# ScalarE casts one half of batch 0's last values, and the first 600 items of an attention-and-MLP kernel stand in a new order

## The chip, the cores and the metric

The kernel runs on one core of a Trainium2 chip. The core has five engines that run side by side, each with its own queue of instructions: TensorE (PE in the profile, its weight loads PEld), VectorE (DVE), ScalarE (ACT), GpSimd (POOL) and SyncE (SP), which here only issues transfers. An engine works through its queue in order; an instruction that waits for another engine or for a transfer holds up everything behind it on its own engine. The metric is the time of the whole program on the chip in microseconds (us), as the median of several runs.

## The reference: what is computed

Attention of 4 batches with 8 heads, 768 positions and head size 64, followed by a two-layer MLP over the 3,072 resulting rows of 512 numbers.

```python
scores = q @ k.T / sqrt(64)          # per batch and head
# retrieval heads (0, 2, 6): causal mask
# the other five heads: causal, and the key is one of the first 4 (sinks)
#                       or at most 63 positions back (window)
a = softmax(scores masked)
x = (a @ v), heads side by side       # 3072 x 512
h = x @ w_in                          # 512 -> 2048
g = max(h, 0) + alpha * min(h, 0)
out = g @ w_out                       # 2048 -> 512
```

Inputs and output are 32-bit floats; the kernel multiplies in bf16.

## The kernel before

**Segments.** A segment n (0 to 15) is one pair of heads of one batch: batch n // 4, pair n % 4 of (2, 6), (1, 5), (0, 4), (3, 7). Each half hh (0 or 1) of a segment is one head. The MLP works on 8 token tiles t (512 and 256 rows of each batch in turn), so t = 0 and 1 belong to batch 0, 2 and 3 to batch 1, and so on.

**Items.** The program is a list of 1,076 named items, `ORDER`, written out at the top of the file. The last loop of the kernel calls them one by one, and this alone sets the order of instructions on every engine's queue. No scheduler moves anything. The names, with the engine that does the work:

- `Lq`, `Lk`, `Lv` n: loads of queries, keys and values. SP issues them, apart from a few. Four buffers each, so a load waits until the segment four before it has been cast.
- `Cq`, `Ck`, `Cv` n: casts to bf16. The strings `CQ`, `CK`, `CV` name the engine by segment (P for POOL, A for ACT, V for DVE). Segment 3's values are cast by halves, `Cv3.0` and `Cv3.1` (`cast_v_head`, line 341 on); for heads that are not retrieval heads `sinks` (line 301 on) then copies the 4 sink rows to the other tiles.
- For n < 8, `Tq`, `Tk` transpose on PE and `tq`, `tk` move the result to `qT` and `kT` (DVE for the first keys, ACT from segment 4 on). For n >= 8, `Dq` (line 322) and `Dk` (line 338) let a transfer do the transpose; SP issues them.
- `S` n.hh.m: scores on PE (lines 413, 423, 430). `s`: the exponential on ACT. `m`: the mask on DVE, where the scores hold none already.
- `A` n.hh: weights times values on PE (line 552). `a`: division by the sum on DVE (lines 562 and 563), into `xn`.
- `X` n: transpose of `xn` into `xT`: on PE with a copy `x` by DVE (line 582) for batch 0 and segment 15, and otherwise by a transfer that SP issues (line 571).
- `P` t.f: first MLP layer on PE (line 597), reading all four parts of `xT` in the order of the pairs. For some, the four are split (`P0.f.0` to `.2`). `p`: relu of the negative on ACT (line 602), into one of three `neg` buffers. `g`: the rest of the activation on DVE (line 609).
- `O` t.s.u: quarter u of the second layer on PE (line 617). `o`: copy by ACT (line 623) and write by a transfer (line 627; POOL issues it for t < 6).
- `wi`, `wo`: loads of the MLP's weights, issued by POOL. `nms`, `nmr`, `nr`, `ns`: masks, made by POOL. `kz`, `vz`, `sz`, `so`, `ro`, `near`, `nz`, `kfz`, `qz`, `vo`, `one`, `zero`: fills, most by DVE. `warm`: matmuls on zeros (line 687).

**Banks.** PE writes to 8 banks. `take` picks the bank at build time, the one given back longest ago among those allowed; an item then waits until the former user's reader (`s`, `p` with `g`, `a`, `tk`, `o`) has let go of it.

**Bursts.** From segment 4 on, score matmuls that stand near one another in the list are collected and emitted together; large bursts alternate between the two halves on the two halves of the array (line 430), small ones use the whole array (line 423).

Of the kernel before, what the change touches and what calls it, by code (L numbers as in the profile page):

```python
# [23 lines left out]
one p0.1 g0.1 P0.2.2 Lq6 Lv7 p0.2 P0.0.2 P1.14 p1.14 g1.2 g1.14 Ck5.0 Ck5.1 nr Tk5 tk5.1 P0.3.2 tk5.0 g0.2 p0.0 g0.0
p0.3 g0.3 P0.12 p0.12 g0.12 p0.13 g0.13 P0.14 kfz1 P1.8 P0.8 wo0 p0.8 g0.8 P0.10 Ck7.1 S5.1.1 s5.1.1 P0.15 p0.15 wo1
wo2 wo3 ns p1.8 g0.15 g1.8 P0.11 p0.11 p0.14 g0.14 p0.10 S5.0.0 Lv5 P0.7 g0.10 P0.6 Ck6.1 P0.4.0 Lq7 P0.4.1 Lk8 Ck6.0
s5.0.0 p0.7 S5.0.2 s5.0.2 Cq4 Tq4 tq4 g0.11 P0.4.2 P0.9 nz0 Ck7.0 S5.1.0 p0.9 g0.9 P1.4 s5.1.0 p1.4 Lv6 S4.0.1 Cq6
m12.1.2 P0.5.0 s4.0.1 P0.5.1 P0.5.2 P1.12 m5.0.0 g1.4 S4.0.3 g0.7 p0.4 p0.5 m5.1.0 g0.4 g0.5 Cv5 P1.10 S5.0.1 p1.10
s5.0.1 near0 p0.6 g0.6 O0.1.0 Tq6 s4.0.3 m4.0.3 Tk6 tk6.1 tk6.0 O0.2.0 P1.6 p1.6 m5.0.1 Tk7 tk7.1 Lv4 S4.0.2 O0.2.1
g1.6 ro1 tq6 p1.12 s4.0.2 tk7.0 O0.1.1 O0.2.2 O0.1.2 g1.10 S4.0.4 S4.0.0 S5.1.2 g1.12 S4.0.5 S4.1.4 S4.1.0 s4.0.4  # L30
s4.0.0 m5.1.1 m4.0.4 s4.1.0 m4.1.0 m5.0.2 O0.1.3 s5.1.2 O0.3.0 O0.2.3 Cq7 m5.1.2 Ck8 Tq7 near1 A5.1 o0.1 S6.1.0 s4.1.4
s6.1.0 O0.3.1 a5.1 s4.0.5 O0.3.2 O0.3.3 m4.0.1 m4.0.5 Cv4 tq7 S7.0.0 S6.0.5 S7.1.1 S4.1.1 Lk9 Lk10 Lq9 o0.2 o0.3
S4.1.3 S7.0.1 A5.0 s4.1.1 s7.0.0 m4.0.0 a5.0 X5 A4.0 s7.0.1 Lk11 s7.1.1 a4.0 s4.1.3 O1.1.0 m4.1.3 Cv7 s6.0.5 m7.0.0
m7.1.1 Lq8 S7.1.0 S6.0.4 S7.0.2 S4.1.5 S6.0.1 S7.1.2 S6.1.1 O1.1.1 Cv6 s7.1.0 O1.0.0 s4.1.5 m7.0.1 s6.1.1 m4.1.5
m6.1.1 s7.1.2 m6.1.0 s7.0.2 m7.0.2 S6.0.2 S4.1.2 S6.1.2 S6.0.0 s6.0.4 s4.1.2 s6.0.1 s6.1.2 O1.0.1 m6.0.5 m7.1.0 m4.1.1
m4.1.4 m7.1.2 m6.1.2 S6.0.3 A4.1 s6.0.0 m6.0.0 m6.0.1 A7.1 O1.1.2 A6.1 s6.0.3 m6.0.4 m6.0.3 s6.0.2 a4.1 a6.1 A6.0 A7.0
a6.0 O1.1.3 O0.0.0 O0.0.1 O0.0.2 O1.0.2 m10.0.2 O1.0.3 O0.0.3 o0.0 X4 X6 a7.1 a7.0 X7 P2.9 P2.3 p2.9 P3.4 Ck9 Cq9 g2.9
P2.14 p2.14 g2.14 Cq8 p3.4 Lq10 Lq11 Dk8.0 P2.10 p2.10 Dk9.1 o1.0 p2.3 g2.3 g3.4 Dk8.1 P3.2 P3.14 P3.12 P2.8 Dq8 P2.1
P3.8 o1.1 p3.2 Dk9.0 Lv10 g2.10 Dq9 p3.14 P2.7 Ck10 g3.2 p3.12 g3.12 g3.14 P2.2 p2.2 g2.2 Cq10 Dq10 P2.11 p2.1 g2.1
p2.11 p2.8 g2.11 P3.6 P2.5 p2.5 g2.5 P2.13 p2.13 g2.8 g2.13 P2.0 p2.0 g2.0 p2.7 P3.0 p3.0 P2.4 S8.0.5 Lv8 Lv11 P2.15  # L40
P2.12 s8.0.5 Cq11 g3.0 p2.15 g2.7 g2.15 S8.0.0 p2.12 g2.12 Ck11 p3.6 S9.0.2 P2.6 p2.6 g3.6 s8.0.0 p2.4 g2.4 g2.6
s9.0.2 p3.8 P3.10 g3.8 p3.10 O3.0.0 O2.0.0 S8.1.5 s8.1.5 O3.0.1 O2.0.1 g3.10 m8.0.0 Cv8 S8.1.3 S9.0.0 S8.0.3 S9.1.1
S8.0.1 S9.1.0 s8.1.3 s9.1.0 s8.0.1 s9.0.0 s8.0.3 m8.0.3 m8.0.1 O2.0.2 O2.0.3 o2.0 Dk10.1 Lv9 m9.0.0 Cv9 m8.0.5 Dk11.0
m9.1.0 m9.0.2 S8.0.4 S9.0.1 S10.1.1 S8.1.4 Dq11 s8.1.4 Lq13 Lk13 O3.0.2 Dk10.0 s9.1.1 s10.1.1 s9.0.1 s8.0.4 O3.0.3
o3.0 Dk11.1 S10.1.0 S10.1.2 m9.0.1 S11.0.2 S9.1.2 S8.0.2 S11.0.0 s9.1.2 Cv10 m9.1.1 A9.0 s11.0.2 s10.1.0 O2.3.0 m9.1.2
A9.1 a9.0 a9.1 X9 s10.1.2 s11.0.0 O2.3.1 Lq15 Lv14 Lq12 S8.1.0 S11.0.1 S10.0.3 m10.1.0 s8.0.2 S10.0.1 S8.1.2 S8.1.1
S10.0.0 O2.3.2 s8.1.2 s8.1.0 m8.1.4 Cq13 s11.0.1 s8.1.1 m11.0.2 m10.1.2 m8.0.4 m11.0.0 A8.0 s10.0.0 m8.1.5 m10.1.1
O2.3.3 a8.0 S11.1.2 S10.0.4 S11.1.0 S10.0.5 S10.0.2 m8.1.3 m11.0.1 s10.0.3 s10.0.1 S11.1.1 s11.1.2 A10.1 s11.1.1
O2.2.0 O2.1.0 s10.0.4 m6.0.2 m10.0.1 Cv11 m8.1.1 m8.1.0 a10.1 m10.0.4 Ck13 m10.0.0 m11.1.2 A11.0 A8.1 O2.1.1 s10.0.2
s10.0.5 o2.3 s11.1.0 Dk13.0 m11.1.1 m10.0.3 m10.0.5 m11.1.0 A10.0 a11.0 a8.1 a10.0 O3.1.0 A11.1 Cq12 O2.2.1 O2.2.2  # L50
O2.2.3 a11.1 X8 O2.1.2 O3.1.1 O3.1.2 X10 o2.2 O3.1.3 O2.1.3 X11 P4.11 o2.1 P4.14 P5.14 p5.14 P4.4 P4.6 Lk12 P5.0 g5.14
Ck12 p4.4 p4.6 p4.11 P4.13 g4.6 p4.14 g4.11 Lq14 g4.14 P5.12 P4.5 P4.12 p4.13 Dq12 o3.1 p5.0 g4.13 Cq14 g5.0 Dk13.1
p4.5 g4.5 g4.4 Cv14 P4.9 p4.9 g4.9 P4.2 P5.2 Dq13 p5.12 g5.12 P4.10 p5.2 P4.8 P4.1 p4.12 g4.12 g5.2 p4.10 g4.10 Lv15
Dk12.0 Dk12.1 Lv12 p4.1 Lk14 Lv13 Lk15 g4.1 P4.7 P4.0 p4.2 g4.2 p4.8 g4.8 p4.0 p4.7 g4.7 P4.15 Cv12 S13.0.1 s13.0.1
S12.0.5 S12.0.3 P4.3 P5.4 g4.0 s12.0.3 p4.3 s12.0.5 S12.1.5 S12.0.1 S12.0.0 S13.1.1 s13.1.1 Dq14 g4.3 Cq15 Ck14
m12.0.3 O4.3.0 s12.1.5 s12.0.1 O4.3.1 O4.3.2 s12.0.0 p4.15 g4.15 P5.6 P5.10 S12.1.1 S12.0.4 S12.0.2 p5.4 S13.1.0 g5.4
p5.6 s12.0.4 Dk14.0 P5.8 s13.1.0 s12.0.2 p5.8 s12.1.1 m12.0.0 g5.6 O4.3.3 Ck15 p5.10 g5.8 m12.0.1 g5.10 m12.0.4 O5.1.0
Cv13 O5.1.1 O5.1.2 o4.3 Dk14.1 S14.1.1 S14.0.0 S12.1.4 S14.0.1 S14.1.0 S13.0.2 m12.1.1 s14.1.0 s13.0.2 O4.2.0 m12.0.5
A12.0 s14.0.1 s12.1.4 O5.1.3 Dk15.1 s14.1.1 Dk15.0 s14.0.0 a12.0 m14.0.1 Dq15 o5.1 O4.2.1 S13.1.2 S12.1.2 S14.1.2
S14.0.4 m13.1.0 m14.0.0 m13.0.1 S14.0.5 S13.0.0 O4.2.2 O4.2.3 s13.1.2 m13.1.2 m13.1.1 s13.0.0 s14.0.4 s14.0.5 m13.0.2  # L60
S12.1.0 m12.1.5 s14.1.2 S12.1.3 S15.0.0 S14.0.3 m13.0.0 A13.1 o4.2 s12.1.0 s12.1.2 A13.0 s15.0.0 O5.0.0 s12.1.3
s14.0.3 m14.0.4 Cv15 a13.1 O5.0.1 a13.0 S15.0.1 S15.0.2 m12.1.0 S15.1.0 S15.1.2 S15.1.1 S14.0.2 O4.1.0 s15.0.2 s15.1.0
m12.1.4 s14.0.2 s15.1.1 m14.1.1 m14.0.5 m14.1.2 m12.1.3 m14.1.0 A12.1 m14.0.3 A14.1 A14.0 a14.0 s15.1.2 a14.1 m15.0.2
s15.0.1 a12.1 O4.1.1 X13 O4.0.0 O4.0.1 O4.0.2 O4.0.3 m15.0.0 m15.1.1 O4.1.2 m15.0.1 m15.1.2 m15.1.0 A15.0 o4.0 A15.1
a15.0 O4.1.3 a15.1 O5.0.2 X15 O5.0.3 X14 x15 o4.1 o5.0 X12 P6.11 p6.11 P6.2 P6.15 P6.10 p6.10 P7.4 P6.0 P6.1 g6.11
g6.10 p6.1 P6.6 P7.8 p6.15 g6.15 g6.1 p6.0 g6.0 P6.5 p7.4 p6.5 p6.6 g7.4 g6.6 g6.5 P6.3 P6.12 P7.2 p6.3 p6.12 g6.12
p6.2 g6.2 P6.4 p7.8 P7.6 P6.14 g6.3 g7.8 p7.6 p6.4 g7.6 g6.4 P7.10 P6.7 P6.8 p6.8 p6.7 P7.0 P6.9 P6.13 g6.7 p7.2 g7.2
g6.8 p7.10 g7.10 p6.9 P7.14 O6.3.0 P7.12 p6.13 g6.13 p7.12 O6.0.0 O6.0.1 O6.1.0 p7.0 g7.0 g6.9 O6.3.1 O7.0.0 O6.3.2
O6.1.1 p7.14 p6.14 g6.14 g7.12 O6.3.3 o6.3 O6.0.2 O6.1.2 O6.1.3 o6.1 O6.0.3 o6.0 O6.2.0 O6.2.1 O6.2.2 O7.0.1 O7.0.2
O6.2.3 o6.2 m12.0.2 g7.14 L2 l2 O7.0.3 o7.0 L0 L1 l1 warm1 l0  # L70
""".split()


@with_exitstack
def kernel(
    ctx: ExitStack,
    tc: tile.TileContext,
    q: bass.AP,
    k: bass.AP,
    v: bass.AP,  # L80
    is_retrieval: bass.AP,
# [7 lines left out]
    nc = tc.nc  # L89
    B, H, S, D = q.shape  # L90
# [73 lines left out]
    NF, NK, NV, NR, NS = 4, 4, 5, 2, 3  # L164
# [175 lines left out]

    def cast_v_head(n, hh):
        vv = vb[n % NV]
        cast_of("PV"[hh])(vv[:, :, hh, 0:D], vf[n % NF][:, :, hh, :])  # L343
        sinks(n, vv.rearrange("p t h c -> p h t c"), [hh], (nc.gpsimd.tensor_copy, nc.vector.tensor_copy)[hh])

    def cast_v(n):
        vv = vb[n % NV]
# [499 lines left out]
```

## Time and profile before

| what | value |
|---|---|
| median of 3 runs | 228.47 us (227.57 to 230.39) |
| the profiled execution's own time | 229.76 us |
| its span, first to last instruction | 228.1 us |
| PE busy | 220.6 us (97%) |
| PE weight loads busy | 136.9 us (60%) |
| DVE busy | 151.5 us (66%) |
| ACT busy | 139.3 us (61%) |
| POOL busy | 46.2 us (20%) |
| PE P L597, share of the chain that ended last | 36% |
| PE P L617, share of it | 35% |
| PE P L552, share of it | 7% |
| granted clock of TensorE | 1.000 |

The time of an execution is a little longer than its span, since starting and ending the program count. Starts in the profile's views are microseconds from the span's start. In a row of the timeline the columns are start, duration, engine, line of the kernel, operation, tiles written and read, shapes, count, and in brackets the idle time ahead with what ended it. The letter q behind an engine's name stands for its queue, where transfers are issued. "A wait of PE" below is time in which PE's next instruction could not start.

### The profile page before, as it was taken

To read this page: it belongs to the slowest core of one execution; us is meant where nothing else is said; L and a number is where in the kernel's file an instruction comes from. 1 tells how busy PE (TensorE), PEld (TensorE's weight loads), DVE (VectorE), ACT (ScalarE), POOL (GpSimd) and SP (SyncE) were. 2 spreads that over 40 slices of the span, in tenths; PEclk is the share of its full clock that TensorE was granted. 3 is DMA by queue.
4 is the path that set the end of the run, shared out by engine and by line. 5 is a ranking of instruction groups with operands and counts; after the bars stand their busy time and mean duration, and the time that the engine had idled before them with its cause. 6 is when DMAs were issued, how large, how long until landed. Compare 5 with 4: busy or idle time off the path is not lost.

```text
span 228.1 us, 5213 instructions
## 1 busy us (share of the span) xinstructions
PE 220.6 (97%) x1977; PEld 136.9 (60%) x2005; DVE 151.5 (66%) x395; ACT 139.3 (61%) x284; POOL 46.2 (20%) x91
## 2 busy tenths in 40 slices
PE   7999979999999999999999999999999999999994
PEld 7989766476455656555556455556556555664454
DVE  5799757996549816999699219987586535966000
ACT  3688448899989128477994136787594236563311
POOL 5689736901040001000400001000110110000000
PEclk9999999999999999999999999999999999999999
DMA  6999999999998799989969899995921420000213
GB/s 193 312 249 219 278 224 280 198 196 244 203 262 165 97 188 207 212 190 188 251 155 194 197 251 174 211 158 107 132 93 38 116 95 0 0 4 0 89 68 120
DMA packets 95417, 37.39 MB, mean 164 GB/s; under 512 B 82440, under 2 KB 93600, under 8 KB 95392
## 3 DMA queue, kind: packets, MB, share of 16 engines
q1 hardware_dynamic: 89136, 27.73, 60.5%
q0 software_dynamic: 5792, 8.93, 17.4%
q10 hardware_dynamic: 464, 0.40, 0.5%
q8 instruction: 15, 0.25, 0.4%
q14 instruction: 10, 0.08, 0.1%
HBM read 27.71 MB, written 6.29 MB: 149 GB/s over the span
## 4 chain that ended last, share of the span: by engine, by line
PE 96%; DVE 2%; issue 1%; DVEq 0%
PE P L597 36%; PE P L617 35%; PE P L552 7%; PE P L430 4%; PE P L413 3%; PE P L687 3%; PE P L363 2%; PE P L636 2%; PE P L423 1%; DVE vb L343 1%; PE P L501 1%; PE P L577 1%; PE P L361 1%; PE P L462 0%; DVE xT L582 0%
## 5 line engine op out<-in xcount | busy, mean ns | idle before, releaser
L609 DVE SCALAR_TENSOR_TENSOR g<-neg,oma,P 128x256 bf16<-128x256 f32 (+1 forms) x128 | 70.9, 608 | 36.5 <-ACT neg L602 36.0
L597 PE MATMUL P<-xT,w_in_b 128*128 128x256 bf16 (+1 forms) x501 | 85.7, 325 | 0.6
L617 PE MATMUL P<-w_out_b,g 128*128 128x512 bf16 x351 | 83.1, 379 | 1.0 <-issue 0.2
L602 ACT ACTIVATE neg<-P 128x512 f32<-128x512 f32 x96 | 54.2, 600 | 26.3 <-PE P L597 18.2
L597 PEld LDWEIGHTS <-w_in_b 128*128 128x128 bf16 x512 | 49.5, 98 | 32.3 <-DVE g L609 0.2
L617 PEld LDWEIGHTS <-g 128*128 128x128 bf16 x368 | 33.9, 98 | 37.3 <-issue 1.0
L469 ACT ACTIVATE eR<-P 128x448 bf16<-128x448 f32 (+4 forms) x63 | 36.8, 633 | 5.8 <-PE P L430 2.5
L623 ACT COPY ot<-P 128x512 f32<-128x512 f32 x23 | 13.9, 605 | 37.1 <-PE P L617 32.3
L627 POOL DMA_DIRECT2D out_dram<-ot x18 | 10.3, 574 | 114.7 <-ACT ot L623 114.6
L517 ACT ACTIVATE eS<-P 128x352 bf16<-128x352 f32 x45 | 20.7, 487 | 3.4 <-PE P L430 3.0
L563 DVE TENSOR_TENSOR xn<-P,rcp 128x448 bf16<-128x448 f32 (+1 forms) x32 | 19.4, 608 | 1.1
L528 DVE TENSOR_TENSOR eS<-eS,ms_near 128x352 bf16<-128x352 bf16 x45 | 14.4, 334 | 0.6 <-ACT eS L517 0.5
L479 DVE TENSOR_TENSOR eR<-eR,mr_near 128x128 bf16<-128x128 bf16 (+5 forms) x54 | 10.8, 229 | 4.7 <-ACT eR L469 4.5
L562 DVE RECIPROCAL rcp<-P 128x7 f32<-128x7 f32 (+1 forms) x32 | 6.3, 197 | 10.1 <-PE P L552 9.9
L552 PE MATMUL P<-vb,eS 128*128 128x65 bf16 x260 | 10.8, 193 | 1.6 <-DVE vb L343 1.4
L552 PEld LDWEIGHTS <-eS 128*128 128x128 bf16 x260 | 9.6, 97 | 4.1 <-issue 2.5
L413 PE MATMUL P<-qT,kT 128*128 128x192 bf16 (+14 forms) x68 | 11.2, 251 | 0.2 <-DVE kT L386 0.2
L430 PE MATMUL P<-qT,kT 64*128 64x176 bf16 (+10 forms) x168 | 10.5, 251 | 0.0
L552 PE MATMUL P<-vb,eR 128*128 128x65 bf16 x276 | 10.5, 193 | 0.0
L430 PEld LDWEIGHTS <-kT 64*128 64x128 bf16 x168 | 6.7, 94 | 6.2 <-issue 5.5
L552 PEld LDWEIGHTS <-eR 128*128 128x128 bf16 x276 | 9.5, 97 | 1.3
L645 DVE COPY ot<-P 128x128 f32<-128x128 f32 x1 | 0.3, 291 | 14.3 <-PE P L636 14.3
(95 smaller groups left out, 180.1 us busy)
## 6 DMA issues: line engine op xcount, KB each, us to landing
out_dram<-ot POOLq DMA_DIRECT2D x18, 256.0 KB, 3.5
kf<-in_k_dram SPq DMA_DIRECT2D x21, 192.0 KB
qf<-in_q_dram SPq DMA_DIRECT2D x18, 192.0 KB
vf<-in_v_dram SPq DMA_DIRECT2D x14, 196.0 KB
qf<-in_q_dram SPq DMA_DIRECT2D x7, 384.0 KB
vf<-in_v_dram SPq DMA_DIRECT2D x12, 192.0 KB
w_in_b<-in_moe_w_in_dram POOLq DMA_DIRECT2D x8, 256.0 KB, 9.5
w_out_b<-in_moe_w_out_dram POOLq DMA_DIRECT2D x4, 512.0 KB, 12.2
```

The source lines that it names most:

```text
L413: nc.tensor.matmul(to, keys, queries, start=True, stop=stop)
L430: nc.tensor.matmul(to, keys[own], queries[own], start=True, stop=True)
L469: nc.scalar.activation(ebuf[n, hh][:, lo:hi].rearrange("p (x c) -> p x c", x=len(parts)), P[:, got[0]:got[0] + len(parts), 0:(hi - lo) // ...
L517: nc.scalar.activation(slots, sc[:, 0:352].rearrange("p (s c) -> p s c", c=176), AF.Exp, scale=scale)
L528: nc.vector.tensor_tensor(slots, slots, ms_near[:, 0:2, :] if m == 0 else ms_near[:, 1:3, :], op=ALU.mult)
L552: nc.tensor.matmul(pav[:, i, :], e[:, o:o + 128], vv[:, j, hh, 0:D + 1], start=(m == 0), stop=(m == len(terms) - 1))
L563: nc.vector.tensor_tensor(xn[n][:, 0:nt, D * hh:D * hh + D], pav[:, :, 0:D], rcp.to_broadcast([128, nt, D]), op=ALU.mult)
L597: nc.tensor.matmul(psg[:, w * i:w * (i + 1)], w_in_b[:, c, 128 * fb:128 * (fb + 1)], xT[:, c, o:o + w], start=(x == 0), stop=(x == 3))
L602: nc.scalar.activation(neg[t, f], bank(held["P", t, f][0]), AF.Relu, scale=-1.0)
L609: nc.vector.scalar_tensor_tensor(g_buf[t % 2][:, fb, 0:w], neg[t, f][:, c], oma[:, fb:fb + 1], bank(got[0])[:, c], op0=ALU.mult, op1=ALU.add)
L617: nc.tensor.matmul(bank(held["O", t, s][0]), g_buf[t % 2][:, f, 128 * s:128 * (s + 1)], w_out_b[:, f, :], start=(f == 0), stop=(f == 15))
L623: nc.scalar.copy(ot, bank(got[0]))
```

## The change

`Cv3.1`, the cast of the second half of segment 3's values, goes from VectorE to ScalarE, and with it the copy of that half's sink rows. The first half stays on GpSimd.

```diff
     def cast_v_head(n, hh):
         vv = vb[n % NV]
-        cast_of("PV"[hh])(vv[:, :, hh, 0:D], vf[n % NF][:, :, hh, :])
-        sinks(n, vv.rearrange("p t h c -> p h t c"), [hh], (nc.gpsimd.tensor_copy, nc.vector.tensor_copy)[hh])
+        copy = cast_of("PA"[hh])
+        copy(vv[:, :, hh, 0:D], vf[n % NF][:, :, hh, :])
+        sinks(n, vv.rearrange("p t h c -> p h t c"), [hh], copy)
```

The first 600 of the 1,076 items are the same items in another order; from the 601st on (`S8.1.4 Dq11 s8.1.4 Lq13 ...`) the list is unchanged. The order of the loads and transposes on SP's queue stays the same throughout. The stretches that the prediction speaks of, in the new order (first the start, then the end of batch 0's attention, then the middle of the first MLP phase, then the end of batch 1's attention, then the MLP of batch 1 with the first scores of batch 2):

```diff
+La zero busy warm4 warm0 sz0 ro1 vz2 Lq0.0 Lq0.1 Lk1 Lq1 Lk0 qz0 kz1 sz1 id kz0 Cq0.0 Tq0.0 Lk2 Ck0.0 Tk0.0 tk0.0 nmr
+warm2 Ck1.0 Cq0.1 Lv0 Lq2 tq0.0 kz2 S0.0.0 Lk3 Ck1.1 s0.0.0 kz3 Tk1 S0.0.1 s0.0.1 Cq1 warm6 warm7 Tq1 nms vz1 Ck0.1
...
+S3.1.1 x1 S3.0.1 s3.0.1 Ck4.1 s3.1.1 X2 x2 P0.1.0 A3.0 a3.0 P0.3.0 P0.1.1 P0.3.1 Cv3.1 A3.1 P0.0.0 m14.0.2 P0.0.1
+P0.2.0 P0.2.1 a3.1 X3 Tq5 tq5 Lq6 Lv7 Tk4 nz1 x3 P1.2 near0 P1.0 P0.1.2 tk4.0 p1.2 g1.2 wi3 near1 one nr p1.0 P0.3.2
...
+g0.13 p0.14 P0.10 p0.12 p0.15 Ck5.1 Ck6.0 g0.15 Ck5.0 Tk5 P0.11 tk5.1 tk5.0 P0.8 g0.12 wo0 wo1 wo2 Ck7.1 p0.10 g0.10
+P1.8 p1.8 P0.4.0 p0.8 S5.0.2 near2 s5.0.2 P0.4.1 P0.4.2 g0.14 P0.9 p0.11 g1.8 g0.8 wo3 S5.1.1 s5.1.1 g0.11 Ck6.1 p0.9
+Lv5 S5.1.0 p0.4 Lq7 Lk8 Lv6 P0.5.0 P1.12 ns Cq4 nz0 Tq4 s5.1.0 g0.9 Cv7 p1.12 tq4 g1.12 S5.0.0 s5.0.0 Cq6 P0.5.1
...
+S6.1.1 m7.0.1 s6.0.1 S6.0.0 m7.1.1 m6.0.1 s7.1.0 S4.1.2 S6.0.3 s6.0.3 m6.0.3 O1.1.3 O1.0.0 O1.0.1 s7.0.2 s6.1.1 Cv6
+s6.0.0 m6.0.0 m4.1.5 s4.1.2 m6.1.1 A4.1 m7.1.0 A7.1 m7.0.2 A7.0 X5 s6.0.2 s6.1.2 m6.1.2 A6.1 a4.1 Lk11 A6.0 O0.0.0
+O0.0.1 a6.1 O0.0.2 O0.0.3 a6.0 a7.0 O1.0.2 Lq8 a7.1 Cq8 X4 Ck9 X6 O1.0.3 X7 P2.2 P2.8 Lq10 Lq11 o0.0 P2.11 o1.0 Dk8.0
+p2.8 g2.8 P2.10 p2.10 p2.2 o1.1 P3.8 p3.8 g2.10 g3.8 P2.7 g2.2 P2.13 P2.5 p2.7 g2.7 p2.13 g2.13 p2.11 p2.5 g2.5 g2.11
+Dk9.1 Dk8.1 Dq8 Dk9.0 Ck10 P3.14 P2.4 p2.4 Cq10 g2.4 P2.9 p3.14 g3.14 S8.0.5 P2.3 p2.3 P2.6 p2.6 g2.6 P2.1 p2.1 g2.3
+Lv10 Dq9 Dq10 S9.0.2 p2.9 g2.9 g2.1 P3.0 p3.0 s8.0.5 P3.12 s9.0.2 P2.0 P3.10 g3.0 p3.12 P3.2 g3.12 p3.10 p2.0 Ck11
```

The same five stretches before:

```diff
-vz2 id busy warm4 warm0 warm5 vz0 qz0 Lq0.0 sz2 so2 Lq0.1 zero vz3 nms Lk1 Lq1 sz1 Cq0.1 nmr Ck1.1 kz1 La Lk0 Ck1.0
-kz0 Cq1 Cq0.0 Tq0.0 Ck0.0 Tk0.0 tk0.0 Lk2 Ck2.0 Lv0 warm2 tq0.0 S0.0.0 s0.0.0 qz S0.0.1 Tk1 warm3 warm6 vo kz2 Ck0.1
...
-a2.1 X2 x1 x2 m8.1.2 near2 Ck4.0 P0.0.0 wi2 s3.0.1 A3.0 Cv3.1 P0.3.0 a3.0 P0.2.0 P0.2.1 A3.1 Ck4.1 Lk7 Lk6 P0.1.0
-P0.1.1 P0.0.1 Tk4 tk4.0 Cq5 m14.0.2 a3.1 X3 nz1 tk4.1 x3 Tq5 P0.3.1 tq5 P1.2 p1.2 P1.0 p1.0 g1.0 P0.1.2 wi3 P0.13 Lq4
...
-s5.0.0 p0.7 S5.0.2 s5.0.2 Cq4 Tq4 tq4 g0.11 P0.4.2 P0.9 nz0 Ck7.0 S5.1.0 p0.9 g0.9 P1.4 s5.1.0 p1.4 Lv6 S4.0.1 Cq6
...
-m4.1.4 m7.1.2 m6.1.2 S6.0.3 A4.1 s6.0.0 m6.0.0 m6.0.1 A7.1 O1.1.2 A6.1 s6.0.3 m6.0.4 m6.0.3 s6.0.2 a4.1 a6.1 A6.0 A7.0
-a6.0 O1.1.3 O0.0.0 O0.0.1 O0.0.2 O1.0.2 O1.0.3 O0.0.3 o0.0 X4 X6 a7.1 a7.0 X7 P2.9 P2.3 p2.9 P3.4 Ck9 Cq9 g2.9
...
-p2.11 p2.8 g2.11 P3.6 P2.5 p2.5 g2.5 P2.13 p2.13 g2.8 g2.13 P2.0 p2.0 g2.0 p2.7 P3.0 p3.0 P2.4 S8.0.5 Lv8 Lv11 P2.15
-P2.12 s8.0.5 Cq11 g3.0 p2.15 g2.7 g2.15 S8.0.0 p2.12 g2.12 Ck11 p3.6 S9.0.2 P2.6 p2.6 g3.6 s8.0.0 p2.4 g2.4 g2.6
```

## The prediction

> **What bounds the kernel now.** I read the page first: the busy row of the matmul engine over 40 slices, then the chain that ended last.
>
> ```profile
> PE   7999979999999999999999999999999999999994
> PE 96%; DVE 2%; issue 1%; DVEq 0%
> ```
>
> TensorE (PE) is the bound. In the first half one slice stands out, the sixth (28.5 to 34.2 us), and the 2% of DVE in the chain is one cast. So only a wait of PE is worth anything, and any new wait of PE costs its full length. After 110 us, in the part of the order that the change leaves as it is, PE's rows have gaps of at most 0.43 us, so a delay at 110 us is carried to the end.
>
> Second, the timeline of VectorE (DVE), GpSimd (POOL) and PE around that slice. Columns: start, duration, engine, line, operation, tiles.
>
> ```profile
> 26.79 2.62 DVE L343 CAST vb<-vf 128x448 bf16<-128x448 f32 x1
> 29.44 0.36 DVE L306 COPY vb<-vb 4x192 f32<-4x192 f32 x1
> ...
> 27.00 0.52 POOL L328 CAST natm<-kf 128x384 bf16<-128x384 f32 x1
> 27.45 0.84 POOL L315 CAST natq<-qf 128x768 bf16<-128x768 f32 x1
> 28.22 0.91 POOL L288 MEMSET natk<- 128x960 f32 x1
> ...
> 26.45 0.56 PE L552 MATMUL P<-vb,eS 128*128 128x65 bf16 x13
> 26.84 1.24 PE L597 MATMUL P<-xT,w_in_b 128*128 128x512 bf16 x5
> 29.46 0.22 PE L552 MATMUL P<-vb,eS 128*128 128x65 bf16 x2 [1.38 <-DVE vb L343]
> 29.86 0.49 PE L552 MATMUL P<-vb,eS 128*128 128x65 bf16 x11 [0.18 <-DVE vb L306]
> ```
>
> The cast of segment 3's second half of values (item Cv3.1) took 2.62 us on DVE while POOL ran without a break. A DVE cast nearly as large, later and with POOL idle, is short:
>
> ```profile
> 46.23 0.62 DVE L328 CAST natm<-kf 128x384 bf16<-128x384 f32 x2
> ```
>
> Two in 0.62 us. PE waited: from the first of A3.1's 13 weight loads (27.71) to the item behind them are 2.45 us, against 0.58 for A3.0, the same 13 matmuls. The stall is 2.45 - 0.58 = **1.87 us**.
>
> Third, the queue of SyncE (SP), which I read because the new order asks for the scores of batch 2 sooner:
>
> ```profile
> 75.02 5.59 SPq L571 DMA_TRANSPOSE xT<-xn  x3
> 80.71 2.29 SPq L212 DMA_DIRECT2D qf<-in_q_dram  x4
> 83.10 4.65 SPq L338 DMA_TRANSPOSE kT<-natk  x3
> 87.84 1.24 SPq L322 DMA_TRANSPOSE qT<-natq  x1
> 89.13 1.34 SPq L338 DMA_TRANSPOSE kT<-natk  x1
> 90.53 0.57 SPq L246 DMA_DIRECT2D vf<-in_v_dram  x1
> 91.14 1.24 SPq L239 DMA_DIRECT2D vf<-in_v_dram  x1
> 92.43 1.00 SPq L242 DMA_DIRECT2D vf<-in_v_dram  x1
> 93.47 3.45 SPq L322 DMA_TRANSPOSE qT<-natq  x2
> ```
>
> The last of the three xT transposes (X7) is issued at 79.39. From there SP issues back to back until Dq9, the transpose of segment 9's queries (93.47, the first of the last row): no idle time over 0.1 us. When Dq9's data is complete, the GB/s of the transfers tells (93 to 98 us, 40 slices of 0.125 us):
>
> ```profile
> GB/s 189 197 199 189 209 264 172 129 225 228 221 217 229 215 213 215 223 205 223 217 223 240 98 4 96 287 91 0 0 0 0 104 211 229 219 203 199 209 156 33
> ```
>
> The stream stops after slice 27, at 96.4, and starts again with Dq10. So Dq9 is there at **96.4**. The scores S9.0.2, which read it, came far later, as the 128x448 group at 101.5:
>
> ```profile
> 99.81 1.89 PE L597 MATMUL P<-xT,w_in_b 128*128 128x512 bf16 x8
> 101.53 0.55 PE L423 MATMUL P<-qT,kT 128*128 128x448 bf16 x4
> ```
>
> **The change part by part, against the profiled execution's own 229.76 us** (span 228.1). The median of the runs, 228.47, is 1.29 lower; I add the difference to the median.
>
> *The cast on ScalarE (ACT).* It removes 2.62 + 0.36 from DVE and adds a 128x448 cast and a 4-partition copy to ACT. ACT's row for a 128x384 cast of the same types is 0.51, so 0.51 x 448/384 = 0.60; the copy lies between ACT's smallest copies (0.18) and DVE's 0.36; I take 0.3. ACT is idle for 5.23 us just there (26.36 to 31.58, in its timeline "5.23 <-PE P L363"), so 0.9 us is hidden; without that cover it would cost at most 0.9. Cv3.1 then ends at 26.3 + 0.9 = 27.2, and A3.1's turn on PE is at about 27.8: the stall is gone with 0.6 to spare. Next late is the path A3.1, its normalisation on DVE (0.86), X3, x3: with 0.3 us from PE to DVE, x3 ends at 30.9, and P1.2 starts at 30.7 instead of 32.14. That keeps 1.44 of the 1.87, since before, the items behind the stall ran without gaps.
>
> *The start.* The warm-up matmuls ahead of the first transposes drop from 40 to 36 (0.11 each there), so the transposes start about 0.4 earlier. But two small groups of warm-ups stand later instead (4 x 0.055 each), POOL does nms (five operations, 1.45) and kz3 ahead of Ck0.1, and ACT's exponentials (0.82 to 0.92 each) set the pace from 13 to 18 us. By hand I get S2.0.1 at 17.8 to 17.9, before 17.83. Taken as 0, bounds -0.4 and +0.3.
>
> *The order from 31 to 76 us.* P0.9's bank is that of g0.10, which now has ACT's six copies of tk5 (1.9) ahead of it: bank free at 42.9, P0.9's turn at 42.4, 0.4 to 0.5 lost. S5.1.0 and S4.0.2 wait for the evacuation of a score just issued, 0.2 each. The burst of scores before O1.1.3 waits for s7.1.0 on ACT, 0.7. So of 1.44 some 0.3 to 0.8 is left by 73 us; I take 0.5. One cast of DVE, Cv7, moves from 68.8 to 46.5, where its load has just landed: the 256-byte packets on SP's queue, of which Lv7 has 1,624 counted from 38.4, are through at 43.6, and its last completion comes at 44.7. The w_out transfers that slow this load start 0.9 earlier (their queue waits for the memset "one", which DVE reaches sooner), so the load may land at 45.5 to 47.5: 0 to 1 us, taken as 0.
>
> *X7.* A6.0's matmuls ended at 75.9. Now O1.1.3 (0.7) and A7.0 (0.4) stand ahead of them: 75.9 + 1.1 - 0.5 = 76.5. DVE then does a6.0, a7.0 and a7.1, 0.78 each, which before overlapped with PE: 76.5 + 0.3 + 2.4 = 79.2; or X6's issue (2.34 in its row) ends at 77.4 + 2.3 = 79.7. X7 goes out at about 79.5, before 79.39: shift **+0.1**, bounds -1.4 (the whole gain kept) and +0.8. So the gain of the cast is already used up here.
>
> *Scores of batch 2.* Before, S9.0.2 stood behind 22 groups P2/P3 and two small scores counted from P2's first (82.06): 101.54 - 82.06 = 19.48, or 0.86 a group. Now it stands behind 14 groups and one score: 14 x 0.86 + 0.35 = 12.4, due at 94.45. It is moved ahead by 7.1 us and had 101.54 - 96.4 = 5.1 of slack: PE waits 2.0 for Dq9. (S8.0.5 waits for its own queries, complete at 91.5 by the completion writes, about when its turn comes; that is part of the same wait.) Behind the waiting matmul stands all of PE's queue. Since this wait ends with SP's stream, and SP starts it at X7, the total is 2.0 + shift of X7 = 2.1. Against it: Dq9's issue lies 14.1 us behind X7's, of which Lv10's last two are 1.24 and 1.00, while such loads at 102.15 to 104.05 took 0.57 and 0.43; the output writes then in flight now go out earlier. Relief 0 to 1.3; I take 0.7.
>
> Sum: 2.0 + 0.1 - 0.7 = **+1.4 us**, so 231.2 on the profile's scale and 228.47 + 1.4 = **229.9** on the median's.
>
> **Rivals.**
> 1. *Faster.* Dq9 is there in time, and the cast's gain stays: 228.47 - 1.4 = 227.1. It decides at Dq9's landing: it must come by 93.0, 3.4 us earlier. For it: a bare stream (nine transposes at 1.23, loads at 0.45 to 0.6) would be 2 to 3 us shorter. Against: the loads ahead of Dq9 keep the transfers busy whatever SP does. Chance 0.22.
> 2. *Another hold of DVE.* Ck7.1, a cast like Cv3.1, moves from 43.0 to about 41.1, into the middle of POOL's 12 mask operations (ns, 3.6 us long). If it is held to their end at 43.0, DVE loses 1.9, P0.9's bank comes that much later, and the total is 1.4 + 1.9 = 3.3: 231.8. Against: in its old place, beside four of these operations, it took 0.39, alone 0.35. Chance 0.07. [...]
> 3. *Cv7 waits for its load*, 1 us on DVE and then PE: 230.9. Chance 0.06.
> 4. *The change doesn't do what it says*: ACT's cast is late behind s3.1.1, and the stall stays: 229.9 + 1.4 = 231.3. The 5.23 us idle speaks against it. Chance 0.05.
>
> My forecast has 0.60.
>
> **How the numbers follow.** Forecast's own range: -1.4 + 1.3 = about 1.3 below in the kindest case, and +0.7 (shift) +0.7 (no relief) above: 228.5 to 231.4. It and rival 1 have both signs: the range reaches down to 227.0 and up to 232.0, which takes in rivals 2 to 4. Two per cent is 4.6 us (a measurement of this kernel can tell no less from no change). Faster than 223.9 would need more than all of PE's waits ahead of 110 us, about 3.8 with the start: 0.02. Slower than 233.0: rival 2 with the whole wait, or a stall I missed: 0.08. Within: 0.90.
>
> **What would show it.** Right: no DVE cast near 26.8, ACT busy there, A3.1 without a stall, P1.2 near 30.7; X7's issue within 0.8 of 79.4; a PE wait of 1 to 3 us at line 423 near 95, ending as a qT transpose lands. Wrong: X7 well before 78.5, or S9.0.2 without a wait (rival 1); a DVE cast over 1 us near 41 (2) or 46.5 (3); PE idle near 28 (4).

## The result, and the profile after

The changed kernel takes **241.81 us** (median of 6 runs, 238.62 to 245.88) where the kernel before, in the same series, takes 228.68 (227.57 to 230.39). The ratio is 1.0524, with a 95% interval of 1.0469 to 1.0579: slower by 5%. Here and below, a ratio leaves out executions more than 1.5% above the fastest of their kernel (two of these six), while a median holds them all. The forecast was 229.9 with a range of 227.0 to 232.0, a change of under 1%, so the prediction was wrong. The profiled execution took 245.88 us (span 244.2) and is the longest of the six; the other five spans are 236.6 to 242.4. In all six the mean granted clock is below 1 (0.978 to 0.993), so each ran in part at a lower clock; the profiled one shows next where, and the lengths given here are its own. Lines of the changed file are one higher than before (343 is now 344, 597 is 598).

First the page of the changed kernel: PE's busy row, the granted clock, and the chain that ended last.

```profile
PE   8899999933999999979997999999999999999995
PEclk9999999995899999999997999999999999999999
PE 73%; DMA 15%; DVE 4%; SPq 3%; ACT 2%; issue 1%; POOL 1%; DVEq 0%; ACTq 0%
```

Before, the chain was 96% PE and every digit of PE's row but three was a 9. Now two slices (48.8 to 61.1 us) are at 3, with a clock that falls to half in the second of them, and 15% of the chain are transfers. Which ones, the list of the chain's longest pieces tells (start, length, what):

```profile
38.02 18.55 DMA vf<-in_v_dram
```

That is a load of values, the third of the four that make up Lv7; SP begins to issue it at 38.02, and it is complete at 56.57. PE's own waits in the changed kernel (total us, times, longest):

```profile
PE P L424 <- DVE g L610: 7.5, 1, 7.5
PE P L424 <- DMA qT<-natq: 2.4, 2, 1.8
PE P L431 <- DMA kT<-natk: 1.6, 1, 1.6
...
PE P L414 <- DVE qT L288: 0.6, 1, 0.6
PE P L553 <- POOL vb L349: 0.6, 1, 0.6
```

The second row is the wait that the prediction forecast, on two scores. The first is the loss. DVE's timeline around it:

```profile
47.11 0.73 DVE L610 SCALAR_TENSOR_TENSOR g<-neg,oma,P 128x512 bf16<-128x512 f32 x1
56.76 0.63 DVE L349 CAST vb<-vf 128x896 bf16<-128x896 f32 x1 [8.91 <-DMA vf<-in_v_dram]
```

The cast at 56.76 is Cv7. Moved ahead, it now stands in front of g1.12 on DVE and waits 8.91 us for its load. The bank of the score S5.0.1 is the one that g1.12 gives back, so PE stands still from 50.7 to 58.2. Then it pays a second time. PE's busy time and granted clock by stretches of 2 us:

```profile
54.00:56.00 2.00, 0.00 (x0) 0.97 0.58 110
56.00:58.00 2.00, 0.00 (x0) 0.50 0.78 233
58.00:60.00 2.00, 1.30 (x5) 0.50 1.06 241
60.00:62.00 2.00, 2.00 (x15) 0.50 1.03 197
62.00:64.00 2.00, 2.00 (x15) 0.82 1.27 210
```

(The columns are the stretch, its length, PE's busy time and matmuls, the clock, the transfers' share and GB/s.) In stretches of 0.5 us the clock is half from 56.0 to 62.5, and four 128x512 matmuls take 1.86 us there (from 59.15) against 1.03 ahead of the wait (from 47.98). So PE works some 4 us at half speed and loses some 2.0 us, an estimate from these figures.

**Where the 16.1 us of span went.** PE's idle time in all is 18.1 us against 7.5 before (span less busy time, 244.2 - 226.1 and 228.1 - 220.6): 10.6 more. Its busy time is 5.5 higher. Of that, 2.0 are the half clock just shown, and 1.7 a second stretch of it (131.0 to 134.4) behind the 1.6 us wait at line 431. The other 1.8 I can't place.

What the prediction said of the stall is there too. ACT's and PE's timelines of the changed kernel:

```profile
26.99 0.57 ACT L344 CAST vb<-vf 128x448 bf16<-128x448 f32 x1
27.59 0.36 ACT L306 COPY vb<-vb 4x192 f32<-4x192 f32 x1
...
28.12 0.56 PE L553 MATMUL P<-vb,eS 128*128 128x65 bf16 x13
```

A3.1's 13 matmuls run in one piece, and P1.2 starts at 31.3 instead of 32.1.

### The profile page after: what moved, and what is told of

Same layout as the page of the kernel before. It is cut to its first block, busy times and chain, and to the rows that moved or that the text cites. A ratio compares the mean times of both kernels' runs of the same rounds, so it can differ in the third digit from the quotient of the medians.

```text
span 244.2 us, 5245 instructions
## 1 busy us (share of the span) xinstructions
PE 226.1 (93%) x2005; PEld 137.6 (56%) x2005; DVE 150.7 (62%) x393; ACT 141.1 (58%) x286; POOL 45.6 (19%) x91
## 4 chain that ended last, share of the span: by engine, by line
PE 73%; DMA 15%; DVE 4%; SPq 3%; ACT 2%; issue 1%; POOL 1%; DVEq 0%; ACTq 0%
PE P L618 31%; PE P L598 25%; DMA vf<-in_v_dram 8%; PE P L553 6%; PE P L431 3%; DMA kf<-in_k_dram 3%; DMA kT<-natk 3%; PE P L688 2%; DVE g L610 2%; PE P L364 2%; PE P L637 1%; DMA qT<-natq 1%; PE P L414 1%; ACT eR L470 1%; SPq L322 1%
## 5 line engine op out<-in xcount | busy, mean ns | idle before, releaser
L598 PE MATMUL P<-xT,w_in_b 128*128 128x512 bf16 (+1 forms) x512 | 88.6, 329 | 1.2 <-DVE g L610 0.8
L618 PE MATMUL P<-w_out_b,g 128*128 128x512 bf16 x368 | 86.5, 383 | 0.0
L603 ACT ACTIVATE neg<-P 128x512 f32<-128x512 f32 x96 | 55.2, 602 | 38.6 <-PE P L598 25.9
L518 ACT ACTIVATE eS<-P 128x352 bf16<-128x352 f32 x45 | 21.4, 501 | 4.7 <-PE P L431 4.7
L480 DVE TENSOR_TENSOR eR<-eR,mr_near 128x128 bf16<-128x128 bf16 (+5 forms) x54 | 11.8, 247 | 7.0 <-ACT eR L470 7.0
L424 PE MATMUL P<-qT,kT 128*128 128x176 bf16 (+7 forms) x33 | 4.6, 249 | 9.8 <-DVE g L610 7.5
L431 PE MATMUL P<-qT,kT 64*128 64x176 bf16 (+12 forms) x171 | 11.0, 252 | 1.6 <-DMA kT<-natk 1.6
L349 DVE CAST vb<-vf 128x896 bf16<-128x896 f32 x10 | 6.1, 623 | 8.9 <-DMA vf<-in_v_dram 8.9
L553 PEld LDWEIGHTS <-eR 128*128 128x128 bf16 x276 | 10.2, 100 | 2.2 <-issue 1.2
```

The costliest lines, as they stand in the source:

```text
L431: nc.tensor.matmul(to, keys[own], queries[own], start=True, stop=True)
L518: nc.scalar.activation(slots, sc[:, 0:352].rearrange("p (s c) -> p s c", c=176), AF.Exp, scale=scale)
L553: nc.tensor.matmul(pav[:, i, :], e[:, o:o + 128], vv[:, j, hh, 0:D + 1], start=(m == 0), stop=(m == len(terms) - 1))
L598: nc.tensor.matmul(psg[:, w * i:w * (i + 1)], w_in_b[:, c, 128 * fb:128 * (fb + 1)], xT[:, c, o:o + w], start=(x == 0), stop=(x == 3))
L603: nc.scalar.activation(neg[t, f], bank(held["P", t, f][0]), AF.Relu, scale=-1.0)
L618: nc.tensor.matmul(bank(held["O", t, s][0]), g_buf[t % 2][:, f, 128 * s:128 * (s + 1)], w_out_b[:, f, :], start=(f == 0), stop=(f == 15))
```

## The experiments

Two theories stood at first. **A**: Cv7 in its new place waits for its load, and the rest is small. **B**: the loads of the new order come later as a whole, and if Cv7 did not wait, the next reader would. Line numbers are up to two lower than above where a kernel's file is shorter. Of each list of items the diffs show only the few items around a change.

### e1_late_cast: the changed kernel, Cv7 back in its old place

```diff
-g0.9 Cv7 p1.12 tq4 g1.12
+g0.9 p1.12 tq4 g1.12
-a5.0 a4.0 m4.1.3 S6.0.1
+a5.0 a4.0 m4.1.3 Cv7 S6.0.1
```

> The changed kernel with one item moved: VectorE's cast of segment 7's values (Cv7) goes back to its old place, behind the item m4.1.3. Theory A (the cast waits for its load, everything behind it on VectorE and then TensorE waits with it, and the clock is halved for some 4 us afterwards): the 7.9 us wait and the some 2 us of half clock go, 241.8 - 9.9 = 231.9, or less if the later waits for transposes (1.0, 2.3 and 1.8 us) shrink too: 228 to 232.5. Theory B (the loads of the new order come 2 to 3.5 us later as a whole, so that the next reader waits in its place): above 236, with another wait of several us between 50 and 66 us.

Measured: 234.63 us (233.52 to 235.71), ratio 1.0265 (1.0191 to 1.0339), so it stays open whether this order is still 2% slower than the kernel before. One item gives back 7.2 of the 13.1 us. There is no wait between 50 and 66 us, and the granted clock is 1.0 in all four runs. So B falls; but A's 228 to 232.5 is missed by 2 us, and what is left is more than small:

```profile
PE P L423 <- DMA qT<-natq: 1.7, 1, 1.7
PE P L430 <- DMA kT<-natk: 1.1, 1, 1.1
...
PE P L413 <- DVE qT L287: 0.9, 1, 0.9
```

Item by item, the gaps in PE's row of weight loads, which run a little ahead of the matmuls and so show more (in the changed kernel 2.26 us before S9.0.2, where the matmuls show 1.79), are 0.94 us before S8.0.5, 2.16 before S9.0.2, 1.36 before S10.0.3 and 1.08 before S1.0.0. The gaps given below before single items are of this kind. The last two were in no sum of mine; e7 takes them up.

### e2_cast_alone: the kernel before, with only the cast on ScalarE

```diff
-        cast_of("PV"[hh])(vv[:, :, hh, 0:D], vf[n % NF][:, :, hh, :])
-        sinks(n, vv.rearrange("p t h c -> p h t c"), [hh], (nc.gpsimd.tensor_copy, nc.vector.tensor_copy)[hh])
+        copy = cast_of("PA"[hh])
+        copy(vv[:, :, hh, 0:D], vf[n % NF][:, :, hh, :])
+        sinks(n, vv.rearrange("p t h c -> p h t c"), [hh], copy)
```

> The kernel before, with the cast and the copy of the sinks on ScalarE and nothing else changed. My prediction's first step: the 1.87 us stall of A3.1 goes and 1.44 us of it are kept, 228.5 - 1.4 = 227.1. Rival (the 1.4 us are lost again at the wait for a transpose or load further on): 228.5.

Measured: 228.10 us, ratio 0.9991 (0.9963 to 1.0020). No gain, though its trace shows just what was wanted. These are all of PE's waits:

```profile
PE P L688 <- DVE busy L288: 1.2, 1, 1.2
PE P L414 <- DVE kT L387: 0.2, 1, 0.2
```

Its span is 225.8 us, 2.3 below that of the profile before. The spans of the thirteen executions of the kernel before that stand beside it explain the contradiction: eight lie between 225.4 and 226.5, four between 227.3 and 227.5, one at 230.3. The profile of before, at 228.1, is a long execution; e2's ten are 225.3 to 227.0. So the median of the kernel before does not hold much of the stall that its profile shows. That the four at 227.4 are those with a stall is only argued: of nineteen executions taken later, seventeen have spans from 225.6 to 228.8 without such a step between.

### e3_order_alone: the new order with Cv7 late, the cast back on VectorE

The edit is e1's together with e2's in reverse.

> The new order with Cv7 in its old place, and the cast of segment 3's second half back on VectorE. Theory A: what e1_late_cast has, plus 1.4 to 1.9 us if VectorE is held again by GpSimd's work at 27 us; plus 0 to 0.3 if GpSimd is idle there in the new order. Theory B: as e1_late_cast, above 236.

Measured: 237.53 us (233.97 to 239.82, no interval); the profiled span is 235.7. The cast took 0.41 us and its copy 0.37 on DVE: it wasn't held. A3.1 waits 0.7 us in all. The rest above e1 is a longer wait before S10.0.3 (2.50 us) and the half clock behind it: 0.50 from 124 to 126 us, where e1, behind 1.36 us, shows 1.00. So the expected 0 to 0.3 us was missed, but most of these 2.9 us lies at S10.0.3, some 90 us behind the cast. The one execution whose clock stayed at 1.0 took 233.97 us, which is within e1's.

### e4_early_in_old: the kernel before, with only Cv7 moved ahead

```diff
-p0.9 g0.9 P1.4
+p0.9 g0.9 Cv7 P1.4
-m4.1.3 Cv7 s6.0.5
+m4.1.3 s6.0.5
```

> The kernel before with one item moved: Cv7 stands behind the evacuation g0.9 on VectorE, as in the changed kernel. If the early place alone is the fault: 234 or more, with a wait of over 4 us for the load. If it takes the early place and the later load together: the load is complete at 44.7 in the old order and the cast's turn comes at about 46, so 228.5 to 229.5, with a wait under 1 us.

Measured: 237.58 us (236.19 to 238.09), ratio 1.0385 (1.0318 to 1.0452). My own reading, load complete at 44.7, fails for this execution: in the *old* order too the load is not there. DVE's timeline of this run:

```profile
26.18 0.39 DVE L342 CAST vb<-vf 128x448 bf16<-128x448 f32 x1
26.60 0.25 DVE L305 COPY vb<-vb 4x192 f32<-4x192 f32 x1
...
45.73 0.75 DVE L608 SCALAR_TENSOR_TENSOR g<-neg,oma,P 128x512 bf16<-128x512 f32 x1 [0.42 <-ACT neg L601]
54.41 0.63 DVE L347 CAST vb<-vf 128x896 bf16<-128x896 f32 x1 [7.93 <-DMA vf<-in_v_dram]
```

The first two rows are as telling as the last. Cv3.1 took 0.39 us here, not 2.62, and A3.1 did not stall. In the timeline of GpSimd, which takes up work at 26.71 (a load of keys came 0.8 us later than in the first profile), the loads of w_out then go out from 34.89, not 37.35:

```profile
33.54 1.26 POOL L658 TENSOR_SCALAR_AFFINE_SELECT mr_near<-one 128x1248 bf16<-128x1248 bf16 x1
...
34.89 2.27 POOL L695 DMA_DIRECT2D w_out_b<-in_moe_w_out_dram  x3
```

In the first profile POOL had stood idle for 3.62 us ahead of the row "mr_near<-one", which needs the item `one` from DVE, and DVE was late because of the held cast. This gave the third theory. **C**: Lv7 races with w_out. While w_out is absent it moves fast, beside w_out it crawls (610 and 149 packets per us, read under e8), and the profile of before showed the race won only because the very stall that the change takes away had delayed w_out. How far the traces bear out this last part is told point by point below.

### b_again: the kernel before, a second profile

> The kernel before, unchanged: a second profile of it. If the 2.62 us cast on VectorE at 26.8 us was a coincidence of that one execution (GpSimd was in the middle of work there because a load of keys came 0.7 us earlier than in the run e4_early_in_old): the cast takes 0.4 us, A3.1 waits under 0.3 us, and the first w_out load is issued at about 35 instead of 37.35 us. If the hold belongs to the kernel: 2 us or more again, and w_out at about 37.

Measured: 230.33 us, span 227.3. The hold comes again, this time on the copy of the sinks. Timelines of DVE and POOL:

```profile
26.37 0.57 DVE L343 CAST vb<-vf 128x448 bf16<-128x448 f32 x1
26.98 2.07 DVE L306 COPY vb<-vb 4x192 f32<-4x192 f32 x1
...
26.64 0.59 POOL L328 CAST natm<-kf 128x384 bf16<-128x384 f32 x1
27.18 0.82 POOL L315 CAST natq<-qf 128x768 bf16<-128x768 f32 x1
27.95 0.89 POOL L288 MEMSET natk<- 128x960 f32 x1
```

PE waits 1.4 us, and w_out goes out at 36.59. So the hold is no freak, and no constant either: of the four profiles of the old order with the cast on DVE (before, e4, b_again, e8 below) three have it. It ends about when POOL's run of work ends (28.84 here and 29.58 in e8, with DVE free at 29.05 and 29.69).

### e5_w_out_late: the changed kernel, w_out's loads 5.8 us later

```diff
-g0.12 wo0 wo1 wo2 Ck7.1
+g0.12 Ck7.1
-g0.8 wo3 S5.1.1
+g0.8 S5.1.1
-ns Cq4 nz0 Tq4
+ns Cq4 nz0 wo0 wo1 wo2 wo3 Tq4
```

> The changed kernel with the four loads of w_out moved on GpSimd behind the mask work ns, the cast Cq4 and the clearing nz0 (from 36.5 us to some 43 to 46 us), and nothing else. Theory C (segment 7's values are late because w_out's transfers take turns with them packet by packet): Cv7 waits under 1 us, the half clock at 56 to 62 us is gone, and only a quarter of w_out may be missed by O0.2.0 for up to 2 us: 234.5 to 237. Theory D (the load is late because SyncE issues it late, whatever w_out does): Cv7 still waits over 5 us, 239 or more.

Measured: 237.10 us (236.69 to 240.10), ratio 1.0430 (1.0360 to 1.0500). In total this is 0.1 past C's range, but the wait itself decides, and it is gone. DVE's timeline:

```profile
46.21 0.73 DVE L609 SCALAR_TENSOR_TENSOR g<-neg,oma,P 128x512 bf16<-128x512 f32 x1
46.87 0.61 DVE L348 CAST vb<-vf 128x896 bf16<-128x896 f32 x1
```

Cv7 starts at 46.87 without a wait. D falls: SP's third issue for Lv7, which lasted 4.17 us in the changed kernel, takes 1.58 here, so its length follows w_out and is no cause of its own. The price is paid elsewhere: w_out itself is late, and PE waits for it and for what stands behind it.

```profile
PE P L617 <- DMA w_out_b<-in_moe_w_out_dram: 2.1, 1, 2.1
```

PE's gaps are 1.59 before O0.2.0 and 2.39 before O0.2.3, beside gaps like those of e1.

### e8_masks_first: e4 with 3.6 us of masks in front of w_out

```diff
-P0.8 wo0 p0.8
+P0.8 ns wo0 p0.8
-wo3 ns p1.8
+wo3 p1.8
```

> e4_early_in_old (old order, Cv7 early, 237.6) with GpSimd's mask work ns, 3.6 us long, put in front of the four w_out loads, which then go out at 38.5 to 41 instead of 34.9 us. Theory C, with a cliff (while w_out is absent the load of segment 7's values moves some 500 packets of 256 bytes per us, beside w_out some 155): 3.6 us are enough for nearly all 1,624 packets, Cv7 waits under 1 us, 228.5 to 230. If the load's end only shifts by about as much as w_out does (3.6 us): Cv7 still waits 4 us or so, 233 to 235. If w_out is not the cause in the old order: 7.9 us again, 237.

Measured: 229.22 us, ratio 1.0017 (0.9979 to 1.0055), against 237.58 for e4. It is a cliff. DVE's and POOL's timelines:

```profile
27.35 2.34 DVE L305 COPY vb<-vb 4x192 f32<-4x192 f32 x1
...
49.17 0.62 DVE L347 CAST vb<-vf 128x896 bf16<-128x896 f32 x1
...
40.62 3.01 POOL L695 DMA_DIRECT2D w_out_b<-in_moe_w_out_dram  x4
```

The hold of 2.34 us came on top of the masks, so w_out went out 5.7 us later than in e4, not 3.6; how few would have been enough stays open. Cv7 does not wait. In the old order the early Cv7 costs nothing (1.0017) once w_out leaves the load alone.

The counts of the transfers' packets show the two regimes. q1 is SP's queue, q0 that of w_out. First the kernel before from 38.25 to 40.25 us, then the changed kernel from 45.5 to 52:

```profile
q1 hardware_dynamic: 1219, 0.52, 122.4%
q0 software_dynamic: 1, 0.00, 0.0%
```

```profile
q0 software_dynamic: 1034, 1.03, 93.0%
q1 hardware_dynamic: 967, 0.26, 28.8%
```

Alone, in the first stretch, SP's queue moves 610 packets per us (1,052 of the 1,220 in that view are under 512 bytes); beside w_out, in the second, 149 (967 / 6.5), nearly one for one with w_out's 1,034, whose packets are four times as large (1.03 MB against 0.26). That the two take turns packet by packet, as C has it, was my guess: the counts of this stretch agree with it, but no view shows the turns themselves. The counts don't agree everywhere: from 41 to 45 us in the changed kernel SP's queue moved only 225 packets beside 675 of w_out, and why, no run shows.

### e6_scores_late and e7_four_repairs: what else the order costs

e6 is e1 with the two scores moved back:

```diff
-p3.14 g3.14 S8.0.5 P2.3
+p3.14 g3.14 P2.3
-Dq9 Dq10 S9.0.2 p2.9
+Dq9 Dq10 p2.9
-p3.0 s8.0.5 P3.12 s9.0.2 P2.0
+p3.0 P3.12 P2.0
-p3.2 S8.1.5 s8.1.5
+p3.2 S8.0.5 S9.0.2 S8.1.5 s8.0.5 s9.0.2 s8.1.5
```

> e1_late_cast (234.6) with the scores S8.0.5 and S9.0.2 and their exponentials moved back, in front of S8.1.5. Their waits for transposes (0.94 and 2.16 us) go. S10.0.3 waits for a transpose that stands behind Dq11, and Dq11 waits for VectorE's cast Cq11, which comes behind evacuations and so shifts with TensorE: then the 3.1 us are kept, 231.5. If that transpose comes by the load stream alone, S10.0.3's wait grows by what is saved: 234.6.

Measured: 231.29 us (228.43 to 236.78), ratio 1.0085 (1.0038 to 1.0132): 3.3 below e1, where 3.1 was expected, though with this spread the close agreement may be luck. S10.0.3 still waits 1.12. The reason stands in SP's queue, here of e1:

```profile
103.81 1.22 SPq L337 DMA_TRANSPOSE kT<-natk  x1
109.10 1.21 SPq L321 DMA_TRANSPOSE qT<-natq  x1
...
112.77 3.54 SPq L337 DMA_TRANSPOSE kT<-natk  x2
```

and in its list of waits:

```profile
SPq L321 <- DVE natq L314: 4.0, 1, 4.0
```

SP issues nothing from 105.0 to 109.1. It waits for `natq`, the cast Cq11 on DVE, and behind this wait stands Dk10.0 (112.77), which S10.0.3 reads. Before, that transpose at line 321 went out at 105.48 and Dk10.0 at 109.13. Cq11 is one of the last items that the change moved: at 99.7 us before, at 108.5 in e1. e7 puts it back, and `qz` too:

```diff
-p2.0 Ck11 p3.2
+p2.0 Ck11 Cq11 p3.2
-Lv9 Dk11.0 Cq11 S9.1.0
+Lv9 Dk11.0 S9.1.0
-Ck1.1 s0.0.0 kz3
+Ck1.1 s0.0.0 qz kz3
-S1.1.0 qz s1.1.0
+S1.1.0 s1.1.0
```

> e6_scores_late with two more items moved: VectorE's cast Cq11 ahead, behind Ck11 (in the new order it stands 9 us later than in the old one), so that SyncE is not held 4.1 us at Dq11 and S10.0.3's 1.36 us wait goes; and the clearing qz of a query tile ahead, behind s0.0.0, so that S1.0.0 does not wait 1.1 us for it. 231.5 - 1.4 - 0.6 = 229.5. If other waits take their place: 231.5.

Measured: 229.87 us, ratio 1.0056 (1.0025 to 1.0088). Neither S10.0.3 nor S1.0.0 waits. With these put back (Cv7, the two scores, Cq11 and `qz`), 11.9 of the 13.1 us are back; what stays is some 0.6%. No version here beats the kernel before; e2 comes nearest, as fast as it.

## Why the prediction was wrong, point by point

**The step that failed** is the sentence on Cv7: "its load has just landed ... 0 to 1 us, taken as 0". It cost 7.5 us of PE's time and some 2.0 us of half clock. I had it as rival 3, with the right mechanism, at a price of 1 us and a chance of 0.06. Three things led to it.

- *The landing was read from one execution.* It was read well: by the completion writes that the traces keep, the last of Lv7's four loads ended at 45.0 in that profile (the prediction has 44.7). But in the old order it ended at 46.4 in b_again, which has the hold too and w_out at 36.59 (this lies within the 45.5 to 47.5 that the prediction allowed for such a shift), and at 54.5 in e2 and 54.2 in e4, where DVE is not held, `one` comes sooner and w_out goes out at 35.06 and 34.89 instead of 37.35. In the old order, then, the early landing is seen only where the hold, or e8's masks, delayed w_out.
- *Only one side of the race was moved.* w_out did go out 0.9 us earlier in the changed kernel, at 36.47, as forecast; but its packets come in at the same time in both profiles. It is Lv7 that is late there: its first packet starts at 39.6 instead of 38.4, a shift that the prediction did not consider. First the kernel before, then the changed one: all packets from 38.25 to 40.75 us, where those under 512 bytes are nearly all Lv7's, and w_out's from 40.25 to 40.75.

```profile
DMA packets 1507, 0.62 MB, mean 247 GB/s; under 512 B 1313, under 2 KB 1506, under 8 KB 1506
q0 software_dynamic: 24, 0.02, 32.9%
```

```profile
DMA packets 1076, 0.83 MB, mean 330 GB/s; under 512 B 517, under 2 KB 1075, under 8 KB 1075
q0 software_dynamic: 15, 0.01, 17.1%
```

  Of Lv7's 1,624 packets 1,258 were through by 40.75 before, and 464 in the changed kernel. Whether the new order makes Lv7 late is open: in e5, with the same order of loads, its first packet starts at 38.4.
- *The landing was moved in proportion.* The traces show two outcomes and nothing between. In four of the eleven profiles (before, b_again, e5, e8) over 1,000 packets were through when w_out's came in, and Lv7 ended between 44.1 and 46.4; in the other seven at most some 500 were, and it ended between 54.2 and 56.6. By the rates above, 794 packets that miss the fast stretch cost 794 / 149 - 794 / 610 = 4.0 us, an estimate. The changed kernel lost 11.6, in part in the slow stretch from 41 to 45 us that the rates do not explain.

**The half clock** was in no term. A wait of PE was priced at its own length; here 7.5 us cost some 9.5.

**The cast on ScalarE.** Right in mechanism and size: 0.57 + 0.36 against 0.60 + 0.3 estimated, hidden in ACT's idle time; the stall of A3.1 is gone. P1.2 starts at 31.3 instead of the 30.7 forecast, because A2.0 now waits 0.6 us for a cast of values on POOL and the start lost a little. Wrong in what it is worth: I took 1.44 us off the median, but the median has little of it (e2, 0.9991). "I add the difference to the median" presumes that the profiled execution differs from the median one by a constant. It seems to have differed by the very stall in question.

**The start**, taken as 0 within -0.4 and +0.3: S1.0.0 waits 0.6 to 1.1 us for `qz`, which the change moves behind S1.1.0. S2.0.2 starts 0.5 us later in e1 than in e2. A term a little outside its bounds.

**P0.9** was to lose 0.4 to 0.5 us for its bank: 0.46 in e1.

**X7** was to go out at about 79.5: 79.38 in e1 (89.76 in the changed kernel, behind the stall). Right.

**S9.0.2 and S8.0.5** were forecast to wait 2.1 us together, less a relief of 0.7. They wait 1.03 and 2.26 in the changed kernel, 0.94 and 2.16 in e1, and e6 confirms 3.3. The mechanism was right and the size twice too small. I had Dq9 there at 96.4 + 0.1 - 0.7 = 95.8 and PE at 94.45. In e1 Dq9 went out at 93.63 against 93.47 before, so the relief of 0.7 that the sum took off did not come, and S9.0.2 started at 96.8; less the 3.1 us of waiting, PE would have been there at 93.7. Each end of the difference was off by 0.7 to 1 us, in the same direction.

**The tail.** I said that behind 110 us a delay is simply carried to the end. It isn't: Cq11, among the last of the moved items, holds SP for 4 us, and PE meets this at S10.0.3, where the order is long the old one again. In the changed kernel that is 1.85 us, and 1.7 more by the clock.

**Rival 2** (Ck7.1 held while POOL makes masks) did not show: the cast of keys on DVE at 41.46, in the middle of POOL's masks (39.46 to 42.93), took 0.40 us in the changed kernel. Rivals 1 and 4 are ruled out by the S9.0.2 wait and by A3.1.

By the terms that e1, e6 and e7 measured, the order without Cv7's move costs some 6 us, so the forecast of 229.9 would have been wrong even with the one step mended.

## What to carry to other kernels

When a change moves a reader ahead to "just behind" its load, ask what else is on the transfer queues at that time, who starts it, and when the load's own packets start: with a large load on a second queue the landing was here a race with two outcomes, some 10 us apart (44.1 to 46.4 and 54.2 to 56.6 us), and the place must be safe in the worse one. A profile of one execution shows one outcome of every race in it; a stall seen in it is worth what it costs on the median, and removing it also moves everything that it had delayed. Where the reordered part of a list ends, look for the transfers that still wait for its last casts.

## What the runs showed of the hardware

**The granted clock after a wait.** In the changed kernel it falls to 0.50 about 5.2 us after PE's last matmul (50.7 to 55.9) and comes back about 4.5 us after matmuls resume (58.2 to 62.7); in e4 the two take 3.6 us (49.1 to 52.7) and 3.5 us (56.1 to 59.6). The ends of these stretches follow from mean clocks: 0.88 in the 0.5 us from 55.5 and 0.79 in the 0.5 us from 62.5, in e4 0.69 in the 2 us from 52 and 0.61 in the 2 us from 58. So neither length was the same in the two runs. For shorter gaps the length does not tell whether half clock follows. In the changed kernel a gap of 1.85 us before S10.0.3 was followed by 3.4 us at half clock (131.0 to 134.4), one of 2.26 before S9.0.2 by none (1.00 from 104 to 112); e3's 2.50 was followed by half clock (0.50 from 124 to 126), e1's 1.36 by none (1.00 from 118 to 126). What decides between such gaps, no run here shows.

**VectorE beside GpSimd.** A 128x448 cast from 32 bits to bf16 or its 4-partition copy took 2.07 to 2.62 us in three profiles and 0.39 and 0.25 in a fourth. In the three the held operation began from 0.21 us ahead of a run of casts and fills on POOL (27.00 in the first profile, 27.46 in e8) to 0.34 us behind its start (26.64 in b_again), and ended 0.1 to 0.3 us after that run. In e4 both operations were over by 26.85, and POOL's run began at 27.98. In b_again the cast, begun 0.27 us ahead of POOL, took 0.57, and the copy behind it 2.07. So in these profiles it was the moment, and not the operation, that set the price.
